# Two changes in a fused attention and feed-forward kernel: how float64 weights become float32, and where the probabilities are split

## The chip, the cores and the metric

One core of a Trainium2 chip. The metric is the device time of the program in microseconds, the median of the runs shown; less is better. The engines named below are TensorE (PE, with its weight loads PEld), VectorE (DVE), ScalarE (ACT), GpSimd (POOL) and SyncE (SP, which issues the DMA transfers).

## The reference, cut to what matters

```python
# q, k, v: [8, 8, 576, 64] float32;  w_a, w_b: [512, 1536], w_out: [1536, 512] float64
k_p = k.reshape(B, H, 72, 8, D).mean(axis=3)      # keys and values pooled by 8
v_p = v.reshape(B, H, 72, 8, D).mean(axis=3)
scores = scale * np.matmul(q, k_p.transpose(0, 1, 3, 2))
scores = scores - np.max(scores, axis=-1, keepdims=True)
attn = np.exp(scores)
attn = attn / (np.sum(attn, axis=-1, keepdims=True) + 1e-09)
x = np.matmul(attn, v_p)                          # heads side by side: [4608, 512]
out = ((x @ w_a) * (x @ w_b)) @ w_out             # [4608, 512] float32
```

The weights reach the chip as float64, so the kernel makes float32 out of their 64 bits itself.

## The kernel before, in words

Every float32 factor on TensorE is split into a high part, rounded to the short float32r format, and a low part, the remainder; a product is three products (high by high, low by high, high by low). So all of TensorE's operands are float32r.

The 4608 rows of x are made in 40 chunks of 128 or 64 queries (`chunk`) and multiplied in nine tiles of 512 rows. A tile takes twelve steps of the inner loop, one for 128 of the 1536 features: `ffn_in` (a and b, 24 products of 512 columns into `psa` and `psb`), `gated` (h = a * b on DVE, L530; split into `hh` on ACT and `hl` on DVE), and one step later `ffn_out` (twelve products into `acc`).

The order is written by hand. Chains of work (generators) are resumed slot by slot, about six slots a step; `yield n` continues n slots later, `yield PE` asks for a turn on TensorE between two groups of the inner loop's products. What one resumption issues goes to the engines' queues in that order, and each engine runs its queue in order.

The weights: `convert_weights` runs once for each of the three matrices and each of the twelve steps, 36 times, while the first tile is multiplied. SP loads the words of a step (`load_words`). ACT makes `low` (L211, the low word scaled) and `mag` (L212, the magnitude of the high word). DVE masks and shifts the high word (L213), puts the sign and the exponent's top bit back (L216), and multiplies by whether the magnitude reaches float32's normal range (L222, a slot later). POOL adds `low` (L226, another slot later). `split_weight`, for all nine tiles, makes the high part on ACT (L238) and the low part on POOL (L171 through `low_part`, tiles `jla`, `jlb`, `jlo`).

The probabilities: a chunk's scores `s` are exponentiated on ACT (L426), summed on DVE (L428, the factor is `z`, L430), and multiplied by `z` on POOL (L432; in two of the first four chunks on DVE). ACT copies the high parts into `pr` and `rem` (L441, L443; of 72 pooled keys 64 are handled pair of heads by pair of heads, the other 8 for four heads at once in `rem`), POOL makes the low parts (L171). `turn` then transposes on TensorE (L477): four transposes of the high half, a slot later four of the low half and two of the rest. ACT takes each of the three groups out of PSUM (L478). A block of chunks is multiplied with the values (L510 to L513, tile `po`), ACT takes the high part (L521) and DVE, a slot later, the low part (L523, in the profile L171 `xl`). Scores, transposes and these products share two PSUM buffers with the tag `att`.

Of the kernel before, what the change touches and what calls it, by code (L numbers as in the profile page):

```python
# [9 lines left out]
F32 = mybir.dt.float32  # L10
# [10 lines left out]
P = 128  # L21
# [6 lines left out]
# the high word of float64 2**-126, read as float32  # L28
MIN_HIGH = 2.0**-15 * 1.125
# [12 lines left out]
# of the pooled keys the first KM are multiplied with the values head pair by head pair, the KR  # L42
# that remain for four heads at a time: (hi, lo, hi) x 4 heads x KR rows
# [23 lines left out]
# the same before the first step: chunks one after the other, the values, the second batch's keys,  # L67
# the weights' loads and how much later their conversion begins
# [45 lines left out]
def attn_moe_kernel(ctx: ExitStack, tc: tile.TileContext, q, k, v, vr, wa, wb, wo, out):  # L114
# [12 lines left out]
    ident0 = tmp("ident0")[:, :P]  # L127
    make_identity(nc, ident0)
    ident = const.tile([P, P], F32R, name="ident")
# [43 lines left out]
    # the first batch's inputs wait where the last weights come later  # L173
# [21 lines left out]
    def convert_weights(name, j, first):  # L195
        """float64 bits to the nearest float32: the sign and the exponent's top bit stay, 27 bits of
        the high word move up by three, what lies below float32's normal range becomes zero, and
        the low word rounds into the last three bits"""
# [6 lines left out]
        for f in range(NF):  # L205
# [480 lines left out]
```

## Time and profile before

| | us |
|---|---|
| median of three runs (1107.82 to 1108.48) | 1107.91 |
| span of the profiled execution | 1107.4 |
| PE busy in it | 1038.7 |
| DVE busy | 611.5 |
| POOL busy | 618.8 |
| ACT busy | 522.9 |

The profiled execution is one run of the program; the span goes from its first to its last instruction. The shares of busy time are means over the whole span. The kernel has two stages with different limits, so the rows below are taken from each stage by itself: an opening of some 216 us, in which the weights are converted and the first tile is multiplied, and the rest.

### The profile page before, as it was taken

The numbers are of one execution on the slowest core, as the hardware profiler recorded it, in microseconds if no ns is written. First come the engines' busy times: TensorE is split into PE (matmuls) and PEld (weight loads), VectorE is DVE, ScalarE is ACT, GpSimd is POOL, SyncE is SP. The second block draws the span as 40 slices with busy tenths as digits, with TensorE's granted clock in tenths as the row PEclk, the third lists the DMA queues.
The fourth block names the chain that finished last, engine by engine and source line by source line (L and its number), as shares of the span: only waits on it lengthen the run. The fifth ranks groups of instructions, "written<-read, shape, count | busy, mean of one in ns | idle before, by whom it ended". The sixth has DMA issues, their size and how long they took to land.

```text
span 1107.4 us, 13650 instructions
## 1 busy us (share of the span) xinstructions
PE 1038.7 (94%) x4964; PEld 861.7 (78%) x4964; DVE 611.5 (55%) x917; ACT 522.9 (47%) x1051; POOL 618.8 (56%) x501
## 2 busy tenths in 40 slices
PE   4378887899999999999999999999999999999998
PEld 4356665688887888888888888888888888888887
DVE  7999999863348333753367335654458343332212
ACT  3655555544445445544455445444445444443332
POOL 6557776655555555555555455554556455554442
PEclk9989888999999999999999999999999999999999
DMA  6454344120023000400021002200211020001001
GB/s 220 128 154 126 105 145 131 48 89 1 1 71 110 1 1 22 148 3 1 1 94 59 1 1 91 82 1 1 69 55 49 1 67 1 1 1 38 1 1 38
DMA packets 29874, 59.59 MB, mean 54 GB/s; under 512 B 7120, under 2 KB 7120, under 8 KB 29808
## 3 DMA queue, kind: packets, MB, share of 16 engines
q1 hardware_dynamic: 29808, 58.73, 16.9%
q8 instruction: 39, 0.64, 0.3%
q14 instruction: 27, 0.22, 0.1%
HBM read 49.28 MB, written 9.44 MB: 53 GB/s over the span
## 4 chain that ended last, share of the span: by engine, by line
PE 81%; DVE 14%; issue 2%; DMA 1%; ACT 1%; POOL 0%; SPq 0%; DVEq 0%; POOLq 0%; ACTq 0%
PE acc L573 9%; PE psa L552 8%; PE psb L552 8%; PE acc L575 8%; PE acc L574 8%; PE psa L554 8%; PE psa L553 8%; PE psb L554 8%; PE psb L553 8%; PE ptr L477 2%; PE psc L406 2%; DVE wo_raw L216 1%; DVE wo_raw L213 1%; DVE wa_raw L222 1%; DVE wb_raw L216 1%
## 5 line engine op out<-in xcount | busy, mean ns | idle before, releaser
L171 POOL TENSOR_TENSOR jlb<-wb_raw,jhb 128x512 fp32r<-128x512 f32 x108 | 142.9, 1323 | 220.9 <-ACT jhb L238 220.9
L530 DVE TENSOR_TENSOR h<-psb,h 128x512 f32<-128x512 f32 x108 | 74.5, 690 | 343.6 <-PE psb L554 340.4
L171 POOL TENSOR_TENSOR jla<-wa_raw,jha 128x512 fp32r<-128x512 f32 x108 | 143.9, 1332 | 143.0 <-ACT jha L238 117.5
L557 ACT COPY h<-psa 128x512 f32<-128x512 f32 x108 | 63.5, 588 | 244.1 <-PE psa L554 235.4
L573 PE MATMUL acc<-jho,hh 128*128 128x512 f32 x432 | 175.5, 406 | 0.0
L552 PE MATMUL psb<-xh,jhb 128*128 128x512 f32 x432 | 172.4, 399 | 2.1 <-DVE h L530 2.1
L552 PE MATMUL psa<-xh,jha 128*128 128x512 f32 x432 | 173.7, 402 | 0.0
L554 PE MATMUL psb<-xh,jlb 128*128 128x512 f32 x432 | 170.0, 393 | 2.4 <-POOL jlb L171 2.4
L553 PE MATMUL psa<-xl,jha 128*128 128x512 f32 x432 | 170.0, 393 | 1.0 <-DVE xl L171 1.0
L554 PE MATMUL psa<-xh,jla 128*128 128x512 f32 x432 | 170.0, 394 | 0.0
L575 PE MATMUL acc<-jho,hl 128*128 128x512 f32 x432 | 170.0, 393 | 0.0
L574 PE MATMUL acc<-jlo,hh 128*128 128x512 f32 x432 | 169.9, 393 | 0.0
L553 PE MATMUL psb<-xl,jhb 128*128 128x512 f32 x432 | 169.6, 393 | 0.0
L171 POOL TENSOR_TENSOR jlo<-wo_raw,jho 128x512 fp32r<-128x512 f32 x108 | 155.1, 1437 | 5.6 <-ACT jho L238 5.6
L171 DVE TENSOR_TENSOR hl<-h,hh 128x512 fp32r<-128x512 f32 x108 | 95.1, 880 | 20.7 <-ACT hh L533 20.6
L533 ACT CAST hh<-h 128x512 fp32r<-128x512 f32 x108 | 67.1, 622 | 72.6 <-DVE h L530 72.6
L554 PEld LDWEIGHTS psb<-xh,jlb 128*128 128x128 f32 x432 | 82.0, 190 | 20.8 <-POOL jlb L171 3.3
L575 PEld LDWEIGHTS acc<-jho,hl 128*128 128x128 f32 x432 | 81.9, 190 | 18.2 <-DVE hl L171 0.3
L554 PEld LDWEIGHTS psa<-xh,jla 128*128 128x128 f32 x432 | 82.1, 190 | 17.8
L552 PEld LDWEIGHTS psb<-xh,jhb 128*128 128x128 f32 x432 | 81.9, 190 | 17.8 <-issue 2.5
L553 PEld LDWEIGHTS psa<-xl,jha 128*128 128x128 f32 x432 | 82.4, 191 | 16.6 <-DVE xl L171 1.5
L552 PEld LDWEIGHTS psa<-xh,jha 128*128 128x128 f32 x432 | 82.2, 190 | 15.3
(92 smaller groups left out, 1776.3 us busy)
## 6 DMA issues: line engine op xcount, KB each, us to landing
out<-y SPq DMA_DIRECT2D x36, 256.0 KB, 2.2
kraw<-in_k SPq DMA_DIRECT2D x28, 288.0 KB, 3.9
vraw<-in_v SPq DMA_DIRECT2D x28, 256.0 KB, 3.1
qraw<-in_q SPq DMA_DIRECT2D x28, 256.0 KB, 3.8
words<-in_wa SPq DMA_DIRECT2D x12, 512.0 KB, 3.7
words<-in_wb SPq DMA_DIRECT2D x12, 512.0 KB, 3.7
words<-in_wo SPq DMA_DIRECT2D x12, 512.0 KB, 3.6
vraw<-in_vr SPq DMA_DIRECT2D x14, 192.0 KB, 2.6
```

The source lines that it names most:

```text
L171: eng.tensor_tensor(out=lo, in0=src, in1=hi.bitcast(F32), op=ALU.subtract)
L216: nc.vector.scalar_tensor_tensor(out=wi, in0=hi, scalar=-(1 << 30), in1=wi, op0=ALU.bitwise_and, op1=ALU.bitwise_or)
L406: nc.tensor.matmul(pt[:n, :2 * hk], qh[:, g, :n], kd[:, g].rearrange("p w e s -> p (w e s)"), start=True, stop=False)
L530: nc.vector.tensor_tensor(out=h, in0=pt, in1=h, op=ALU.mult)
L533: nc.scalar.copy(hh, h)
L552: nc.tensor.matmul(pt, wh[:, c], xh[:, kk], start=(kk == 0), stop=False)
L553: nc.tensor.matmul(pt, wh[:, c], xl[:, kk], start=False, stop=False)
L554: nc.tensor.matmul(pt, wl[:, c], xh[:, kk], start=False, stop=(kk == NK - 1))
L557: nc.scalar.copy(h, pt)
L573: nc.tensor.matmul(acc[c], hh[:, cs], wh, start=(f == 0), stop=False)
L574: nc.tensor.matmul(acc[c], hh[:, cs], wl, start=False, stop=False)
L575: nc.tensor.matmul(acc[c], hl[:, cs], wh, start=False, stop=(f == NF - 1))
```

## The change

The weights: ACT makes `mag` first and then `low`. DVE takes the larger of the magnitude and 2^-15 and scales by 2^-16 (one instruction with one source), masks and shifts the result, a slot later puts the sign in and itself adds `low`. The multiplication by the comparison and POOL's add are gone. The next words are loaded a slot later than before, and the step is marked done a slot earlier.

The probabilities: the multiplication by `z` writes `pr` and three copies of the rest directly, in four instructions, in float32. The casts on ACT and the subtractions on POOL are gone. TensorE transposes float32 with a float32 identity, four transposes and later two. ACT takes the high part out of PSUM, and a slot later DVE subtracts it from the same PSUM tile to give the low part. The identity is no longer cast on DVE.

```diff
-            nc.scalar.activation(mag, hi.bitcast(F32), AF.Abs)
+            nc.scalar.activation(mag, hi.bitcast(F32), AF.Abs)
             nc.scalar.activation(low, lo.bitcast(U32), AF.Copy, scale=2.0**-29)
+            nc.vector.tensor_scalar(out=w, in0=mag, scalar1=TINY, scalar2=2.0**-16, op0=ALU.max, op1=ALU.mult)
             nc.vector.tensor_scalar(
-                out=wi, in0=hi, scalar1=0x07FFFFFF, scalar2=3, op0=ALU.bitwise_and, op1=ALU.logical_shift_left
+                out=wi, in0=wi, scalar1=0x0FFFFFFF, scalar2=3, op0=ALU.bitwise_and, op1=ALU.logical_shift_left
             )
+            yield 1
             nc.vector.scalar_tensor_tensor(
-                out=wi, in0=hi, scalar=-(1 << 30), in1=wi, op0=ALU.bitwise_and, op1=ALU.bitwise_or
+                out=wi, in0=hi, scalar=-(1 << 31), in1=wi, op0=ALU.bitwise_and, op1=ALU.bitwise_or
             )
             if f + 1 < NF:
                 load_words(f + 1)
-            yield 1
-            nc.vector.scalar_tensor_tensor(
-                out=w, in0=mag, scalar=MIN_HIGH, in1=w, op0=ALU.is_ge, op1=ALU.mult
-            )
-            yield 1
-            nc.gpsimd.tensor_tensor(out=wi, in0=wi, in1=low, op=ALU.add)
+            nc.vector.tensor_tensor(out=wi, in0=wi, in1=low, op=ALU.add)
             mark("weight", name, f)
...
-        (nc.vector if first and i % 2 else nc.gpsimd).tensor_tensor(
-            out=s[:n], in0=s[:n], in1=z[:n].unsqueeze(2).broadcast_to([n, H, SP]), op=ALU.mult
-        )
-        yield 1
...
-        nc.scalar.copy(pr[:n, 0], s[:n, :, :KM])
-        for x in (0, 2):
-            nc.scalar.copy(rem[:n, :, x], sr)
-        yield 1
-        low_part(nc.gpsimd, pr[:n, 1], s[:n, :, :KM], pr[:n, 0])
-        low_part(nc.gpsimd, rem[:n, :, 1], sr, rem[:n, :, 0])
+        eng = nc.vector if first and i % 2 else nc.gpsimd
+        eng.tensor_tensor(out=pr[:n], in0=s[:n, :, :KM], in1=zb.broadcast_to([n, H, KM]), op=ALU.mult)
+        for x in range(3):
+            eng.tensor_tensor(
+                out=rem[:n, :, x],
+                in0=s[:n, :, KM:].rearrange("p (r c) s -> p r c s", r=NG),
+                in1=zb.broadcast_to([n, H, KR]).rearrange("p (r c) s -> p r c s", r=NG),
+                op=ALU.mult,
+            )
         mark("probs", i)
+        yield 1
         yield PROBS_GAP
...
+            if x == 0:
+                for g in range(NK):
+                    src = pr[:n, 2 * g:2 * g + 2, :].rearrange("p a s -> p (a s)")
+                    nc.tensor.transpose(ptr[:, g, :n], src, ident[:n, :n])
+                nc.scalar.copy(th[:, :, cs], ptr[:, :, :n])
+                yield 1
+                low_part(nc.vector, tl[:, :, cs], ptr[:, :, :n], th[:, :, cs])
+            else:
+                for r in range(NG):
+                    src = rem[:n, r].rearrange("p a c s -> p (a c s)")
+                    nc.tensor.transpose(ptr[:NR, r, :n], src, ident[:n, :n])
+                nc.scalar.copy(tr[:NR, :, cs], ptr[:NR, :NG, :n])
+                yield 1
+                lo = slice(4 * KR, 2 * 4 * KR)
+                low_part(nc.vector, tr[lo, :, cs], ptr[lo, :NG, :n], tr[lo, :, cs])
```

## Rows read from the trace of the kernel before

**Rows 1.** The page's slices: busy tenths of PE and DVE in 40 equal slices.
```profile
PE 4378887899999999999999999999999999999998
DVE  7999999863348333753367335654458343332212
```

**Rows 2.** Table of stretches: us; busy PE, PEld, DVE, ACT, POOL; PEclk, DMA, GB/s.
```profile
68.00:208.00 140.00, 111.24 (x484) 87.75 (x485) 136.23 (x158) 74.73 (x150) 102.89 (x73) 0.85 0.39 118
...
216.00:1107.40 891.40, 887.51 (x4294) 739.66 (x4294) 409.10 (x659) 408.81 (x820) 473.00 (x381) 1.00 0.11 34
```

**Rows 3.** Timeline of PE, one chunk's transposes: start, us, what.
```profile
728.02 0.46 PE L477 MATMUL ptr<-ident,pr 128*128 128x128 f32 x4
728.31 0.47 PE L573 MATMUL acc<-jho,hh 128*128 128x512 f32 x1
728.62 0.39 PE L574 MATMUL acc<-jlo,hh 128*128 128x512 f32 x1
728.85 0.40 PE L575 MATMUL acc<-jho,hl 128*128 128x512 f32 x1
...
729.79 0.53 PE L477 MATMUL ptr<-ident,pr 128*128 128x128 f32 x4
730.16 0.30 PE L477 MATMUL ptr<-ident,rem 128*96 128x128 f32 x2
730.29 0.47 PE L573 MATMUL acc<-jho,hh 128*128 128x512 f32 x1
730.60 0.39 PE L574 MATMUL acc<-jlo,hh 128*128 128x512 f32 x1
```

**Rows 4.** Table of stretches, transposes (L477) alone, busy PE and PEld.
```profile
216.00:1107.40 891.40, 33.29 (x310) 31.38 (x310) 1.00 0.11 34
```

**Rows 5.** Timeline of DVE, the conversion without POOL beside it.
```profile
46.91 0.42 DVE L213 TENSOR_SCALAR wa_raw<-words 128x512 int32<-128x512 int32 x1
47.37 0.69 DVE L216 SCALAR_TENSOR_TENSOR wa_raw<-words,wa_raw 128x512 int32<-128x512 int32 x1
...
123.40 0.69 DVE L216 SCALAR_TENSOR_TENSOR wb_raw<-words,wb_raw 128x512 int32<-128x512 int32 x1
124.19 0.69 DVE L222 SCALAR_TENSOR_TENSOR wb_raw<-wmag_b,wb_raw 128x512 f32<-128x512 f32 x1
```

**Rows 6.** Timelines of DVE and of POOL, the conversion beside POOL.
```profile
97.56 1.65 DVE L216 SCALAR_TENSOR_TENSOR wo_raw<-words,wo_raw 128x512 int32<-128x512 int32 x1
...
97.19 1.47 POOL L171 TENSOR_TENSOR jlb<-wb_raw,jhb 128x512 fp32r<-128x512 f32 x1
```

**Rows 7.** Table of stretches, DVE of one line: L213, then L216, then L222.
```profile
68.00:208.00 140.00, 24.62 (x28) 0.85 0.39 118
...
68.00:208.00 140.00, 44.04 (x28) 0.85 0.39 118
...
68.00:208.00 140.00, 26.34 (x28) 0.85 0.39 118
```

**Rows 8.** Groups by line and shape, whole span: busy us, mean ns, idle before.
```profile
L171 POOL TENSOR_TENSOR pr<-s,pr 128x512 fp32r<-128x512 f32 x32 | 42.6, 1331 | 4.3 <-ACT pr L441 4.2
L432 POOL TENSOR_TENSOR s<-s,z 128x576 f32<-128x576 f32 x30 | 41.7, 1389 | 54.1 <-DVE z L430 34.9 <-ACT jha L238 19.2
...
L171 POOL TENSOR_TENSOR rem<-s,rem 128x64 fp32r<-128x64 f32 x32 | 12.7, 397 | 0.0
...
L171 DVE TENSOR_TENSOR xl<-po,xh 128x512 fp32r<-128x512 f32 x18 | 12.2, 688 | 10.1 <-ACT xh L521 10.1
...
L171 DVE TENSOR_TENSOR xl<-po,xh 128x256 fp32r<-128x256 f32 x2 | 0.8, 418 | 2.7 <-ACT xh L521 2.7
```

**Rows 9.** Table of stretches, POOL's adds (L226) alone.
```profile
68.00:208.00 140.00, 40.47 (x29) 0.85 0.39 118
```

**Rows 10.** Timelines of DVE and of ACT around 110 us.
```profile
110.31 0.41 DVE L213 TENSOR_SCALAR wo_raw<-words 128x512 int32<-128x512 int32 x1
...
110.41 0.66 ACT L211 ACTIVATE wlow_o<-words 128x512 int32<-128x512 uint32 x1
```

More of the change, by code (lines that the diff above doesn't have):

```diff
@@ L27 @@
 NK = DM // P
-MIN_HIGH = 2.0**-15 * 1.125
+TINY = 2.0**-15
 SCALE = 1.0 / float(D) ** 0.5
@@ L125, in tmp @@
         return sb.tile([P, 512], dtype, tag="tmp", name=name, bufs=NTMP)
-    ident0 = tmp("ident0")[:, :P]
-    make_identity(nc, ident0)
-    ident = const.tile([P, P], F32R, name="ident")
+    ident = const.tile([P, P], F32, name="ident")
+    make_identity(nc, ident)
     raw = {name: const.tile([P, NF, 512], F32, name=f"w{name}_raw") for name in ("a", "b", "o")}
@@ L431, in chunk @@
         yield 1
-        (nc.vector if first and i % 2 else nc.gpsimd).tensor_tensor(
-            out=s[:n], in0=s[:n], in1=z[:n].unsqueeze(2).broadcast_to([n, H, SP]), op=ALU.mult
-        )
-        yield 1
-        yield from wait(("turned", i - 2))
-        pr = sb.tile([P, 2, H, KM], F32R, tag="pr", name=f"pr_{i}")
-        rem = sb.tile([P, NG, 3, 4, KR], F32R, tag="rem", name=f"rem_{i}")
-        sr = s[:n, :, KM:].rearrange("p (r c) s -> p r c s", r=NG)
-        nc.scalar.copy(pr[:n, 0], s[:n, :, :KM])
-        for x in (0, 2):
-            nc.scalar.copy(rem[:n, :, x], sr)
-        yield 1
-        low_part(nc.gpsimd, pr[:n, 1], s[:n, :, :KM], pr[:n, 0])
-        low_part(nc.gpsimd, rem[:n, :, 1], sr, rem[:n, :, 0])
-        mark("probs", i)
+        yield from wait(("turned", i - 2))
+        pr = sb.tile([P, H, KM], F32, tag="pr", name=f"pr_{i}")
+        rem = sb.tile([P, NG, 3, 4, KR], F32, tag="rem", name=f"rem_{i}")
+        zb = z[:n].unsqueeze(2)
+        eng = nc.vector if first and i % 2 else nc.gpsimd
[7 more added lines that the diff above has]
+            )
+        mark("probs", i)
+        yield 1
         yield PROBS_GAP
@@ L454, in chunk @@
         total = sum(flat[c][2] for c in members)
-        if i == members[0]:
-            turned[j] = {}
-        def turn(x):
-            rows = P if x < 2 else NR
-            num = NK if x < 2 else NG
-            if x not in turned[j]:
-                if tile_of[i] < 2:
-                    turned[j][x] = sb.tile([P, num, BLOCK], F32R, tag=f"p{x}", name=f"p{x}_{j}", bufs=1)
-                elif x == 0:
-                    both = sb.tile([P, 2, NK, BLOCK_LATER], F32R, tag="work", name=f"p_{j}", bufs=1)
-                    turned[j].update({0: both[:, 0], 1: both[:, 1]})
-                else:
-                    turned[j][x] = sb.tile([P, NK * BLOCK], F32R, tag="p0", name=f"p{x}_{j}", bufs=1)[
-                        :, :NG * BLOCK_LATER
-                    ].rearrange("p (g s) -> p g s", g=NG)
-            dst = turned[j][x]
-            pt = ps.tile([P, 512], F32, tag="att", name=f"ptr_{i}_{x}", bufs=2)
-            ptr = pt.bitcast(F32R).rearrange("p (g s) -> p g s", g=NK)
-            for g in range(num):
-                src = pr[:n, x, 2 * g:2 * g + 2, :] if x < 2 else rem[:n, g]
-                src = src.rearrange("p a s -> p (a s)") if x < 2 else src.rearrange("p a c s -> p (a c s)")
-                nc.tensor.transpose(ptr[:rows, g, :n], src, ident[:n, :n])
-            nc.scalar.copy(dst[:rows, :, c0:c0 + n], ptr[:rows, :num, :n])
@@ L480, in chunk, with blocks_turned @@
-        yield from wait(("turned", i - 1), ("value", j - 1))
-        for x in range(3):
-            if x < 2 or t < 2:
+        def blocks_turned():
+            if tile_of[i] < 2:
+                both = [sb.tile([P, NK, BLOCK], F32R, tag=f"p{x}", name=f"p{x}_{j}", bufs=1) for x in range(2)]
+                rem = sb.tile([P, NG, BLOCK], F32R, tag="p2", name=f"p2_{j}", bufs=1)
+            else:
+                both = sb.tile([P, 2, NK, BLOCK_LATER], F32R, tag="work", name=f"p_{j}", bufs=1)
+                both = [both[:, 0], both[:, 1]]
+                rem = sb.tile([P, NK * BLOCK], F32R, tag="p0", name=f"p2_{j}", bufs=1)[
+                    :, :NG * BLOCK_LATER
+                ].rearrange("p (g s) -> p g s", g=NG)
+            return (*both, rem)
@@ new lines, in turn @@
+        def turn(x):
+            th, tl, tr = turned[j]
+            cs = slice(c0, c0 + n)
+            pt = ps.tile([P, 512], F32, tag="att", name=f"ptr_{i}_{x}", bufs=2)
+            ptr = pt.rearrange("p (g s) -> p g s", g=NK)
+            if x == 0:
[5 more added lines that the diff above has]
+                low_part(nc.vector, tl[:, :, cs], ptr[:, :, :n], th[:, :, cs])
+            else:
+                for r in range(NG):
[5 more added lines that the diff above has]
+                low_part(nc.vector, tr[lo, :, cs], ptr[lo, :NG, :n], tr[lo, :, cs])
@@ L483, in chunk @@
+        yield from wait(("turned", i - 1), ("value", j - 1))
+        if i == members[0]:
+            turned[j] = blocks_turned()
+        for x in range(2):
+            if x == 0 or t < 2:
                 yield PE
-            turn(x)
-            if x != 1 or t < 2:
-                yield 1
+            yield from turn(x)
         mark("turned", i)
@@ L497, in chunk @@
         per = min(NK, 512 // total)
-        th, tl, tr = (turned[j][x] for x in range(3))
+        th, tl, tr = turned[j]
         for g0 in range(0, NK, per):
@@ L589, in attn_moe_kernel @@
         load_early()
-        nc.vector.tensor_copy(ident, ident0)
         for t in kdiag + vdiag:
@@ L593, in attn_moe_kernel @@
         nc.vector.tensor_reduce(
-            out=mask[:NR], in_=ident0[:NR, :NR].rearrange("p (a c s) -> p c a s", a=3, c=4), axis=AX.XY, op=ALU.add
+            out=mask[:NR], in_=ident[:NR, :NR].rearrange("p (a c s) -> p c a s", a=3, c=4), axis=AX.XY, op=ALU.add
         )
```

## The prediction

> **What bounds the kernel now.** I read the page's slices first, then a table of stretches, then the timelines of single engines inside each stretch.
>
> The slices [rows 1] show two stages. For about the first fifth DVE stands at 9 in nearly every slice and PE wavers between 3 and 9; from there on PE is at 9 to the end and DVE falls to 2 to 7. The table of stretches [rows 2] says it in numbers: from 68 to 208 us DVE is busy 136.2 of 140 us and PE 111.2; from 216 us to the end PE is busy 887.5 of 891.4 us, DVE 409. So the two parts of the change meet two different limits. The weights' conversion lives only in the first stage, where DVE's time (and what makes its instructions long) sets the pace. The turning of the probabilities happens in both, but counts as TensorE time in the second and as DVE time in the first.
>
> What a transpose costs TensorE is read from the timeline of a chunk in the second stage [rows 3]. A 512-column product starts 0.23 us after the one before (728.62 to 728.85). The first four transposes start at 728.02 and the next product at 728.31, so four take 0.29 us, and the product behind them takes 0.31 instead of 0.23: 0.37 us in all. The second visit has four (729.79 to 730.16, 0.37 us) and two more (to 730.29), and again 0.08 us behind: 0.58 us. A mean transpose is thus (0.29 + 0.50) / 10 = 0.079 us. After 216 us there are 310 of them [rows 4], ten a chunk, so 31 chunks; the other nine lie in the first stage.
>
> Why DVE is slow in the first stage is read from single instructions. Undisturbed, the conversion's mask-and-shift (L213) takes 0.42 us and starts its successor after 0.46; the two-operand instructions L216 and L222 take 0.69 [rows 5]. Where an instruction of POOL runs, the same L216 takes 1.65 us, from 97.56, beside a POOL instruction that began at 97.19 [rows 6]. Over 68 to 208 us the three lines take 24.6, 44.0 and 26.3 us for 28 conversions [rows 7], 94.9 us together, where 28 x (0.42 + 0.69 + 0.69) would be 50.4. So 44.5 us are lost beside POOL's 73 instructions [rows 2], 0.61 us for each of them; hl and ql, of the same kind and on the same engine, lose some too, so I take 0.7.
>
> **The change part by part.**
>
> *The transposes, second stage.* Removed: four of ten transposes a chunk, the low half's, with their visit: 0.37 us [rows 3]. The visits of TensorE stay two, four transposes and later two, so the 0.08 us behind each stays as well. If a float32 transpose costs what a float32r one does, that is 31 x 0.36 = 11 us off a stage where PE has no idle time to hide it (0.36, as six of the chunks have 64 rows). No row shows a float32 operand on TensorE. From below I bound it by the cheapest row, 0.29 / 4 = 0.073 us, which brings the gain to 12 us; nothing speaks for less than that. From above I bound it by four times 0.079: the kernel itself splits a float32 operand into two parts, and two such operands make four products. I take the nearest row, the float32r transpose of the same 128 columns and four-byte elements. Two pages of the Trainium skill disagree here: "FP8 and Floating Point Precision", TensorE Precision Notes, gives true float32 four passes through the array, and "TensorE: Matmul & The Clock Gate", Terms, says that on trn2 a transpose mode makes float32 four times faster. By the first the sum would be the rival with four passes below, by the second it is the forecast. No run here shows it yet.
>
> *What goes from ACT and POOL, comes to DVE and waits, second stage.* ACT loses three casts and one of three evictions a chunk, POOL's three instructions of 1.39 + 1.33 + 0.40 us become one of about 1.33 and three of 0.40 [rows 8]. DVE gets two subtractions out of PSUM: the nearest rows are xl's of 128x512 and 128x256, 0.69 and 0.42 us [rows 8], so 1.1 us a chunk. None of this is on the path: DVE is busy 409 of 891 us [rows 2]. I cost it at nothing; the cover is that half-idle DVE. The wait that is added is that a PSUM buffer of the "att" pair comes free only after DVE's subtraction, a slot later. Behind it would queue the next chunk's scores or products on TensorE; but L521 and L523 already give the same buffers back in just this way (ACT, a slot, DVE). If the cover is gone, a wait of one subtraction a visit, 2 x 0.69 x 31 = 43 us, is the far bound; between nothing and that I take nothing, because PE shows no idle time behind the products that do the same.
>
> *The conversion, first stage.* 36 conversions. Removed from DVE: L222. Added to DVE: one single-operand instruction (maximum and scale) and the integer add that POOL had. Undisturbed: before 0.42 + 0.69 + 0.69, after 0.42 + 0.42 + 0.69 + 0.69, so +0.42. In addition the add now stands directly behind the instruction whose result it reads; in such a pair (123.40, 124.19) the second waits until 0.10 us after the first has ended [rows 5], which before was so for a part of the conversions only. I take +0.53 each: 36 x 0.53 = +19 us. Bounds: the new instruction at 0.42 (as L213) or at 0.69 (as the two-operand ones), 15 to 29 us.
>
> Removed from POOL: 36 adds; 29 of them in 68 to 208 us are busy 40.5 us [rows 9]. Each had DVE waiting 0.7 us: -25 us. Bounds: 0.61 each, -22; or all of a POOL instruction's 1.4 us, -50, which would need DVE to be standing at each of them and which the 0.61 contradicts.
>
> The order on ACT is turned so that the magnitude comes first; DVE now needs it at once, where before only the third instruction did. Mostly ACT is ahead. The worst kind is seen at 110.31: L213 starts before L211 (110.41, ending at 111.07), whose place the magnitude takes [rows 10]; DVE would stand 0.76 us, and hl, h and the other matrices' conversions stand behind it in its queue, on which TensorE waits. Six of the 36 conversions are late like this, together 3.6 us: +4. The load of the next words (SP's queue) is issued one slot later, behind the second bit instruction, and the release to the split comes one slot earlier; both move in DVE's own order, and neither is late as long as DVE is the bound: nothing.
>
> *The probabilities, first stage.* Nine chunks x 1.1 us of subtractions out of PSUM come onto the full DVE; adjoining instructions overlap a little, so +9. Two chunks multiply on DVE in four instructions instead of one, +1. POOL has 0.6 us less in each of seven chunks, -2.5. The identity's cast leaves DVE while the first inputs still load: nothing.
>
> Sum of the first stage: +19 - 25 + 4 + 9 + 1 - 2.5 = +5 us. That is a small difference of larger numbers, so I keep -8 to +14 for it. DVE stays the bound: the sum doesn't take it below TensorE's time.
>
> Against the profiled execution, whose span is 1107.4 us: 1107.4 - 11 + 5 = 1101.4; the median of the runs, 1107.91, lies 0.5 above the span: **1102 us**.
>
> **The rivals.**
>
> *Float32 transposes take several passes.* In its favour: the kernel writes float32r wherever TensorE reads, and no row has float32. Against: a transpose only moves data. With p us for one, the second stage changes by 31 x (6p - 0.79); with the +5 of the first stage the change loses from p = 0.105 us on. Two passes, 0.158: +5 + 5 = about 1118 us. Four, 0.316: 31 x (1.90 - 0.79) = +34, and +5, so 1147 us. If only the columns were repeated (0.23 / 4 = 0.057 us each), three more times for six transposes: 31 x 1.03 = +32, less the 11: 1134 us. This is the case that ends slower.
>
> *DVE gets no relief.* Without the adds, POOL's remaining instructions (three splits a step) could meet DVE as often, since DVE now has four instructions for three in the conversion. For it: the added time is of the kind that collides. Against it: POOL's busy time in the stage falls by two fifths. With half of the 25 us lost: 1102 + 12 = 1114 us.
>
> *Full relief.* If POOL's disappearance gives back more than 0.7 us each (1.1), the first stage ends 15 us earlier: 1087 us. Against it the 0.61 measured.
>
> *The removed transposes were hidden.* Then only the +5 remains: 1113 us. Against it stand 887.5 of 891.4 us.
>
> **How the numbers follow.** Forecast (one pass, first stage -8 to +14): 0.64, between 1090 and 1112. Several passes: 0.23, a third of it two passes. No relief: 0.06. Full relief: 0.04. Hidden: 0.03. Two passes, no relief and hidden stay inside a range up to 1127; four passes (0.15) and full relief are left out, so the range is 1090 to 1127. About 0.2%, 2.2 us, is what a measurement of this kernel can tell from no change. Inside the forecast I give 0.48 to faster than 1105.7, 0.10 to within, 0.06 to slower; with full relief faster is 0.52; slower has 0.06 + 0.23 + 0.06 + 0.03 = 0.38; same is 0.10.
>
> **What would show it.** In the profile after: ptr's x4 group followed by a product 0.29 to 0.37 us later (right), or over 0.6 (several passes); PE still full after the first stage; the point from which PE is full within some 10 us of 216; in the first stage L216-like instructions at 1.65 us less often; DVE still the busiest there. Wrong: transposes over 0.105 us, or a first stage that moves by more than 14 us, or idle PE behind "att" in the second stage.

## The result, and the profile after

| | before | after |
|---|---|---|
| median, us | 1107.91 | 1111.01 (1110.71 to 1115.67) |
| ratio to before | | 1.0039, 95% interval 1.0029 to 1.0048 |
| span of the profiled execution, us | 1107.4 | 1113.9 |
| end of the first tile (start of its last gate product on DVE, tile `h`), us | 223.4 | 220.3 |
| from there to the last gate product, us | 874.8 | 884.4 |

The change makes the kernel slower by 0.3 to 0.5%, where 0.5% faster was forecast. The profiled execution after is the longest of seven (1115.67 us), 4.7 us above their median, so its 6.5 us more span overstate a difference of medians of 3.1 us. In every run with both figures the time lies 1.7 to 2.0 us above the span, so the profiled execution of before (span 1107.4) lies some 1.4 us above its own median. The parts are still plain: the first tile ends 3.1 us earlier, and all that follows takes 9.6 us longer.

The page of after, busy tenths of PE and DVE and the granted clock in 40 slices, against [rows 1]:

```profile
PE   4477987899998999999999999999999999999998
DVE  7899999953466344764476445664567444442111
PEclk9788889999998999999999999999999999999999
```

The shape is the same, but PE has a slice of 8 in the thirteenth place, at the same place as a clock of 8: a hole in the stage that was full. The table of stretches (columns as in [rows 2]) shows how big it is:

```profile
68.00:208.00 140.00, 109.73 (x477) 87.00 (x478) 131.97 (x204) 71.06 (x136) 53.98 (x49) 0.88 0.39 119
216.00:1113.90 897.90, 883.60 (x4155) 732.00 (x4153) 444.77 (x714) 368.78 (x694) 459.95 (x412) 0.99 0.11 34
...
332.00:368.00 36.00, 31.01 (x136) 24.13 (x135) 23.54 (x40) 13.43 (x26) 16.73 (x17) 0.91 0.25 83
...
586.00:622.00 36.00, 33.45 (x155) 26.73 (x153) 23.13 (x42) 14.20 (x29) 19.89 (x22) 0.95 0.11 34
...
840.00:876.00 36.00, 33.45 (x167) 26.96 (x166) 23.37 (x44) 14.61 (x29) 20.40 (x22) 1.00 0.10 31
```

From 216 us PE is idle for 14.3 us, where it was 3.9 in [rows 2] (nearly all of it behind the last product). Three stretches hold nearly all that is new: 36 - 31.01 = 5.0 us, and twice 2.55. In two of them the granted clock fell as well: 36 x 0.09 = 3.2 us and 36 x 0.05 = 1.8 us of TensorE's time. Idle and clock together are 15.1 us. Each stretch holds two chunks of 64 rows that follow each other, one at the end of a batch and one at the start of the next. The scores of the first come directly behind the transposes of the 128-row chunk before it, and those of the second, some 15 to 19 us later, directly behind the transposes of the first.

What ends these waits stands in the table of waits after 218 us (us in total, times, longest):

```profile
PE psc L403 <- DVE p L170: 6.4, 5, 1.5
PEld psc L403 <- DVE s L409: 5.0, 6, 0.8
...
PE psc L403 <- DVE s L409: 3.7, 6, 0.6
```

The scores (`psc`) wait for one of the two `att` buffers, which DVE's new subtraction (`p`) still reads, or for the one buffer that is left to be read by the scores' own sum (`s`). The timeline of PE and DVE at the first place shows the order:

```profile
335.83 0.39 PE L561 MATMUL psb<-xh,jlb 128*128 128x512 f32 x1
...
336.06 0.38 PE L481 MATMUL ptr<-ident,rem 128*96 128x128 f32 x2
336.33 0.69 DVE L537 TENSOR_TENSOR h<-psb,h 128x512 f32<-128x512 f32 x1 [3.68 <-PE psb L561]
...
336.94 0.68 DVE L170 TENSOR_TENSOR p<-ptr,p 128x512 fp32r<-128x512 f32 x1
337.77 0.32 PE L403 MATMUL psc<-kdiag,qh 128*64 128x288 f32 x1 [1.32 <-DVE p L170]
...
338.76 0.50 PE L403 MATMUL psc<-kdiag,qh 128*64 128x288 f32 x1 [0.61 <-DVE s L409]
...
340.13 0.63 PE L582 MATMUL acc<-jho,hl 128*128 128x512 f32 x1
340.56 0.63 PE L580 MATMUL acc<-jho,hh 128*128 128x512 f32 x1
...
342.07 0.69 DVE L588 COPY y<-acc 128x512 f32<-128x512 f32 x1 [2.20 <-PE acc L582]
342.80 0.42 DVE L170 TENSOR_TENSOR p<-ptr,p 32x256 fp32r<-32x256 f32 x1
...
343.27 0.35 PE L403 MATMUL psc<-kdiag,qh 128*64 128x288 f32 x1 [0.91 <-DVE p L170]
```

Read it from the top. The last gate product goes to TensorE at 335.83, and right behind it the small transposes (336.06) and the scores, with no product between. DVE executes in order: it must first make `h`, which waits for that last product (3.68 us idle), and only then the subtraction that releases the first buffer. TensorE stands 1.32 us. The small transposes' own subtraction is a slot later again, at 342.80, behind a copy `y` that waits for further products; until then the scores have one buffer, and stand 0.61 and 0.91 us more. The products at 340.13 and 340.56 follow each other by 0.43 us instead of 0.23: after these waits the granted clock is at its lower level (1.2 GHz).

The kernel before has the same small transposes and the same kind of scores, but not side by side. Its timeline of PE for the same two chunks:

```profile
343.16 0.46 PE L477 MATMUL ptr<-ident,pr 128*128 128x128 f32 x4
...
343.45 0.30 PE L477 MATMUL ptr<-ident,rem 128*96 128x128 f32 x2
343.59 0.46 PE L552 MATMUL psa<-xh,jha 128*128 128x512 f32 x1
...
344.81 0.40 PE L554 MATMUL psa<-xh,jla 128*128 128x512 f32 x1
345.04 0.29 PE L406 MATMUL psc<-kdiag,qh 128*64 128x288 f32 x1
```

Between 343.59 and 345.04 stand six products, 1.45 us, in which ACT empties both buffers. The scores here are the second half of that chunk's; the first half came ahead of all its neighbour's transposes, from 339.57 on. In each slot of the inner loop first all chains that are due are resumed, and then one chain that asked with `yield PE` gets the turn. Before, the second visit (low half and small transposes) took that turn, so the scores had to wait for the next slot, six products later. In the change, after the second tile, the small transposes stand behind a `yield 1` and no `yield PE`: they are issued at the start of their slot without the turn, and the next chunk's scores take the turn directly behind them.

### The profile page after: what moved, and what is told of

Same layout as the page of the kernel before. It is cut to its first block, busy times and chain, and to the rows that moved or that the text cites. A ratio compares the mean times of both kernels' runs of the same rounds, so it can differ in the third digit from the quotient of the medians.

```text
span 1113.9 us, 13287 instructions
## 1 busy us (share of the span) xinstructions
PE 1037.6 (93%) x4804; PEld 855.6 (77%) x4804; DVE 640.9 (58%) x1038; ACT 472.9 (42%) x891; POOL 541.7 (49%) x499
## 4 chain that ended last, share of the span: by engine, by line
PE 78%; DVE 17%; issue 2%; DMA 2%; ACT 1%; POOL 0%; SPq 0%; DVEq 0%; POOLq 0%; ACTq 0%
PE psb L559 8%; PE acc L580 8%; PE psb L561 8%; PE psb L560 8%; PE acc L582 8%; PE acc L581 8%; PE psa L559 8%; PE psa L561 8%; PE psa L560 8%; PE psc L403 2%; PE ptr L474 1%; DVE hl L170 1%; DVE wo_raw L223 1%; DVE wb_raw L218 1%; DVE h L537 1%
## 5 line engine op out<-in xcount | busy, mean ns | idle before, releaser
L170 POOL TENSOR_TENSOR jla<-wa_raw,jha 128x512 fp32r<-128x512 f32 x108 | 153.0, 1417 | 120.1 <-ACT jha L235 110.2
L559 PE MATMUL psb<-xh,jhb 128*128 128x512 f32 x432 | 175.7, 407 | 2.1 <-DVE h L537 2.1
L170 DVE TENSOR_TENSOR hl<-h,hh 128x512 fp32r<-128x512 f32 x108 | 106.3, 985 | 9.3 <-ACT hh L540 8.5
```

Source lines behind the costliest of these rows:

```text
L170: eng.tensor_tensor(out=lo, in0=src, in1=hi.bitcast(F32), op=ALU.subtract)
L559: nc.tensor.matmul(pt, wh[:, c], xh[:, kk], start=(kk == 0), stop=False)
```

## The experiments

Every kernel was timed beside the kernel before, which had medians of 1107.77 to 1108.04 us. "First tile" and "rest" are the two last rows of the table above; "idle" is PE's idle time between the end of the first tile and the last product. The rest also holds what a lower granted clock took there: about 5 us in after and e2, 1.7 us in e4, e6 and e9, nothing in the others.

| run | median us | ratio, 95% interval | first tile | rest | idle |
|---|---|---|---|---|---|
| before | 1107.91 | | 223.4 | 874.8 | 0.1 |
| after | 1111.01 | 1.0039 (1.0029 to 1.0048) | 220.3 | 884.4 | 10.4 |
| e1_no_gap | 1105.83 | 0.9979 (0.9971 to 0.9988) | 219.5 | 874.2 | 6.0 |
| e2_probs_only | 1113.84 | 1.0055 (1.0039 to 1.0071) | 220.4 | 881.7 | 8.5 |
| e3_weights_only | 1110.77 | 1.0023 (1.0015 to 1.0032) | 223.8 | 874.9 | 0.1 |
| e4_fp32r | 1110.45 | 1.0029 (1.0019 to 1.0039) | 219.5 | 878.4 | 10.5 |
| e5_act_release | 1110.86 | 1.0022 (1.0014 to 1.0031) | 222.7 | 876.1 | 6.8 |
| e6_two_slots | 1123.66 | 1.0136 (1.0117 to 1.0154) | 228.4 | 882.6 | 11.0 |
| e7_pool_add | 1102.15 | 0.9944 (0.9931 to 0.9957) | 216.3 | 874.9 | 0.0 |
| e8_no_max | 1091.26 | 0.9849 (0.9836 to 0.9863) | 205.0 | 875.3 | 0.4 |
| e9_pool_add_no_gap | 1100.03 | 0.9927 (0.9915 to 0.9939) | 213.9 | 875.7 | 5.9 |
| e10_turn_earlier | 1097.71 | 0.9901 (0.9888 to 0.9914) | 211.5 | 873.7 | 5.6 |
| e11_before_wait | 1109.07 | 1.0013 (1.0003 to 1.0023) | 222.8 | 875.9 | 1.3 |
| e12_only_earlier | 1109.54 | 1.0019 (1.0010 to 1.0028) | 219.1 | 878.2 | 9.7 |

**e1_no_gap: the subtraction without its slot of delay**

```diff
     nc.scalar.copy(th[:, :, cs], ptr[:, :, :n])
-    yield 1
     low_part(nc.vector, tl[:, :, cs], ptr[:, :, :n], th[:, :, cs])
+    yield 1
...
     nc.scalar.copy(tr[:NR, :, cs], ptr[:NR, :NG, :n])
-    yield 1
     lo = slice(4 * KR, 2 * 4 * KR)
     low_part(nc.vector, tr[lo, :, cs], ptr[lo, :NG, :n], tr[lo, :, cs])
+    yield 1
```

> The changed kernel, with DVE's subtraction out of PSUM issued right behind ACT's copy instead of a slot later; nothing is left out. Theory A (TensorE waits for an att buffer that DVE gives back late, because the subtraction stands in DVE's queue behind the gate product, which itself waits for TensorE): TensorE's idle time after 218 us, 14 us in the changed kernel's profile, falls to 3 to 6, the steps at the meeting of two 64-row chunks (third, fifth and seventh tile) lose their 13 to 15 us lengths, and the time is 1097 to 1102 us. Theory B (a float32 transpose costs more than a float32r one): unchanged, 1110 to 1113. Theory C (the first stage got longer through the weights): unchanged as well.

Measured: 1105.83 us, 5.2 below the change, and faster than before. The direction is the one that only the wait explains; the size is less than expected, as 6.0 us of idle time stay. The timeline shows why:

```profile
335.27 0.38 PE L481 MATMUL ptr<-ident,rem 128*96 128x128 f32 x2
335.45 0.34 PE L403 MATMUL psc<-kdiag,qh 128*64 128x288 f32 x1
335.48 0.69 DVE L537 TENSOR_TENSOR h<-psb,h 128x512 f32<-128x512 f32 x1
...
336.20 0.42 DVE L170 TENSOR_TENSOR p<-ptr,p 32x256 fp32r<-32x256 f32 x1
...
336.67 0.35 PE L403 MATMUL psc<-kdiag,qh 128*64 128x288 f32 x1 [0.81 <-DVE p L170]
```

The large subtraction is out of the way, so the first scores start at once; the second ones still meet the buffer of the small transposes, filled 0.2 us before, and wait for its subtraction behind `h`. Issued directly behind ACT's copy, the subtraction still comes too late for scores that stand directly behind the transposes.

**e2_probs_only and e3_weights_only: each part alone.** In e2 the conversion, in e3 the probabilities are those of the kernel before. The core of e2 against the changed kernel; e3 has the same lines the other way round, against the kernel before:

```diff
-            nc.vector.tensor_scalar(out=w, in0=mag, scalar1=TINY, scalar2=2.0**-16, op0=ALU.max, op1=ALU.mult)
...
+            nc.vector.scalar_tensor_tensor(
+                out=w, in0=mag, scalar=MIN_HIGH, in1=w, op0=ALU.is_ge, op1=ALU.mult
+            )
...
-            nc.vector.tensor_tensor(out=wi, in0=wi, in1=low, op=ALU.add)
+            nc.gpsimd.tensor_tensor(out=wi, in0=wi, in1=low, op=ALU.add)
```

> The kernel before with the second part of the change alone (probabilities turned in float32, split on the way out of PSUM); the weights are converted as before. Theory A: the long steps at the meeting of two 64-row chunks are all there, and the first tile's last step, 3 us earlier in the changed kernel, comes at about its time before or up to 9 us later, since DVE gets nine chunks' subtractions without losing POOL's adds: 1112 to 1122 us. Theory B: 1110 to 1118 with transposes of over 0.105 us. Theory C: faster than before, 1098 to 1103.

> The kernel before with the first part of the change alone (weights without GpSimd); the probabilities as before. Theory A: only the first stage moves; by my sum -25 for POOL's adds, +19 for DVE's, +4 for the waits for the magnitude, so -2, and as the changed kernel's profile ends the first tile 3 us earlier with 9 us of subtractions more, rather -8 to -12: 1095 to 1106 us, with the steady part as before. Theory C: 1110 to 1118.

Measured: the probabilities alone bring the loss behind the first tile (881.7 against 874.8, with 8.5 us of idle time at the same three places) and a gain ahead of it (220.4 against 223.4, where about the old time or up to 9 us more was expected). The conversion alone leaves the rest as it was (874.9, idle 0.1), and costs 2.8 us by the medians of its round (1110.77 against 1107.98), where a gain was expected; the time falls into the range of theory C. So there are two losses, of different causes.

**e4_fp32r: the transposes' type.** `rem` and its transposes likewise.

```diff
-        pr = sb.tile([P, H, KM], F32, tag="pr", name=f"pr_{i}")
+        pr = sb.tile([P, H, KM], F32R, tag="pr", name=f"pr_{i}")
-                    nc.tensor.transpose(ptr[:, g, :n], src, ident[:n, :n])
+                    nc.tensor.transpose(ptr.bitcast(F32R)[:, g, :n], src, ident_r[:n, :n])
```

> The changed kernel with the probabilities, their rest and the identity written as float32r and transposed so, which leaves nothing for the low part (the subtraction runs all the same): it leaves out the low part's value and nothing of the work; one cast of the identity on DVE is added in the opening. It prices the type of the transposes by itself. Theory A: within 2 us of the changed kernel, four transposes followed by a product 0.29 to 0.37 us after their start in both. Theory B: 8 us or more below the changed kernel.

Measured: 1110.45 us and 10.5 us of idle time, within 0.6 us of the change by the medians. What float32 itself costs is read off the change's own products. Timeline of PE, the four large transposes, and two small ones of another chunk:

```profile
334.00 0.39 PE L561 MATMUL psb<-xh,jlb 128*128 128x512 f32 x1
334.24 0.60 PE L474 MATMUL ptr<-ident,pr 128*128 128x128 f32 x4
334.59 0.48 PE L559 MATMUL psb<-xh,jhb 128*128 128x512 f32 x1
334.90 0.40 PE L560 MATMUL psb<-xl,jhb 128*128 128x512 f32 x1
...
733.72 0.39 PE L561 MATMUL psb<-xh,jlb 128*128 128x512 f32 x1
733.95 0.38 PE L481 MATMUL ptr<-ident,rem 128*96 128x128 f32 x2
734.09 0.48 PE L580 MATMUL acc<-jho,hh 128*128 128x512 f32 x1
734.40 0.39 PE L581 MATMUL acc<-jlo,hh 128*128 128x512 f32 x1
```

Two products without a visit take 2 x 0.227 us; with four float32 transposes between them they take 0.90, so the visit costs 0.45 us, and the visit of two costs 0.68 - 0.45 = 0.23. With float32r the visit of four costs 0.37, in [rows 3] as in e4. A float32 transpose is thus dearer by about 0.02 us, not twice or four times as dear. By the median visit behind the first tile a chunk costs TensorE 0.45 + 0.23 = 0.67 us where it cost 0.37 + 0.51 = 0.89 (unrounded sums; the second visit in [rows 3], 0.58, is one of the dearer), and in e4 0.37 + 0.19 = 0.56. The type is so worth 0.11 us a chunk, some 3.3 us for 31 of them by these rows; the medians of the runs differ by 0.6 only, with executions of each that lie 5 to 6 us apart.

**e5_act_release: ACT empties the buffer.** The second visit likewise.

```diff
     nc.scalar.copy(th[:, :, cs], ptr[:, :, :n])
+    whole = tmp(f"whole_{i}_{x}").rearrange("p (g s) -> p g s", g=NK)
+    nc.scalar.copy(whole[:, :, :n], ptr[:, :, :n])
     yield 1
-    low_part(nc.vector, tl[:, :, cs], ptr[:, :, :n], th[:, :, cs])
+    low_part(nc.vector, tl[:, :, cs], whole[:, :, :n], th[:, :, cs])
```

> The changed kernel, but ACT copies the whole float32 PSUM tile of turned probabilities to SBUF right behind the copy of the high part, and DVE subtracts from SBUF a slot later, so the att buffer comes free by ACT alone. Theory A (the loss of the second stage is TensorE waiting for an att buffer that only DVE's late subtraction releases): TensorE's idle time after the first tile falls from 10.4 us to below 2, the steps at the three places where two 64-row chunks meet fall back to about 10 us, and the time to 1094 to 1101 us. Rival B (float32 transposes cost several passes): unchanged, 1109 to 1112. Rival C (DVE is the loaded engine and its added subtractions cost the time): unchanged or slower, 1111 to 1114, since DVE keeps every instruction.

Measured: 1110.86 us. No wait for DVE's subtraction is left, but 6.8 us of idle time are. The scores now stand 1.03 us at each of the three places for the second of ACT's two copies, with smaller waits of the same kind 4.0 us in all; the first of the three:

```profile
340.12 0.34 PE L403 MATMUL psc<-kdiag,qh 128*64 128x288 f32 x1 [1.03 <-ACT whole L487]
```

The expectation of under 2 us failed, and with it the first form of the theory, in which DVE's late release was the whole cause. With ACT as with DVE, scores directly behind the transposes wait. The rest did fall to 876.1 us; the first tile, at 222.7, took 2.4 us of that back with the added copies.

**e6_two_slots: a longer delay.** The second visit likewise.

```diff
     nc.scalar.copy(th[:, :, cs], ptr[:, :, :n])
-    yield 1
+    yield 2
```

> The changed kernel with two slots instead of one between ACT's copy and DVE's subtraction out of PSUM; nothing else. Theory A: each att buffer is held about 1.6 us longer, TensorE's idle time after the first tile grows from 10 to 15 to 30 us, and the time goes to 1116 to 1130 us. Rivals B and C (the transposes themselves, or DVE's load): the work of each engine is the same, so 1110 to 1112 us.

Measured: 1123.66 us, inside the expected range, but not for the expected reason: the idle time is 11.0 us, hardly more than with one slot, and 10.5 of them are waits for the scores' own sum `s`, none for the subtraction. The first tile ends at 228.4 instead of 220.3, and the rest takes no longer than in the change (882.6 against 884.4). So behind the first tile the wait hardly grows with the delay; why the first tile does was not followed up.

**e11_before_wait: the late release alone, in the kernel before**

```diff
-            nc.scalar.copy(dst[:rows, :, c0:c0 + n], ptr[:rows, :num, :n])
+            if x != 1 or t < 2:
+                nc.scalar.copy(dst[:rows, :, c0:c0 + n], ptr[:rows, :num, :n])
+                return None
+            return lambda: nc.vector.tensor_copy(dst[:rows, :, c0:c0 + n], ptr[:rows, :num, :n])
...
+        if t >= 2:
+            late()
```

> The kernel before, unchanged in its conversion, its transposes and its splits; only the copy of the turned low half out of PSUM is made by DVE and a slot later, from the third tile on, instead of by ACT at once. This puts the disputed wait into the kernel before by itself. Theory A (an att buffer that DVE releases late makes TensorE wait, at the places where two 64-row chunks meet): TensorE's idle time after the first tile rises from 0.1 to 5 to 15 us, at about 336, 590 and 844 us, and the time to 1113 to 1124 us. Rivals B and C (float32 transposes, or the added subtractions' own time): neither is in this kernel, so 1107 to 1109 us.

Measured: 1109.07 us, idle 1.3 us; 5 to 15 were expected. Only one of PE's waits behind the first tile is for the buffer (`p`):

```profile
PE psc L406 <- DVE p L481: 0.6, 1, 0.6
```

In this kernel, where six products stand between the transposes and the scores and only the low half's buffer is released late, that release costs almost nothing. This miss points to the missing half of the cause.

**e12_only_earlier: the place alone, in the changed kernel**

```diff
-        yield PROBS_GAP
+        yield PROBS_GAP if t < 2 else PROBS_GAP - 1
```

> The changed kernel with one number changed: from the third tile on, a chunk's transposes are issued one slot earlier. DVE's subtraction still comes a slot late and releases the att buffer, the add stays on DVE. Theory A2 (TensorE waits because the small transposes now stand directly ahead of the next 64-row chunk's scores, so that the scores need a buffer that has only just been filled; DVE's late release only lengthens that wait): TensorE's idle time after the first tile falls from 10.4 to 2 to 5 us, with waits for pr the largest part, the three steps of 13 to 15 us fall to 11 or less, and the time goes to 1100 to 1105 us. Theory A in its first form (the late release is enough by itself, wherever the scores stand): idle stays above 8 us and the time at 1108 to 1112 us.

Measured: 1109.54 us, 1.5 below the change. The table of waits of PE behind the first tile:

```profile
PE ptr L474 <- POOL pr L435: 6.0, 4, 2.2
PE psc L403 <- DVE p L170: 3.1, 3, 1.0
```

The scores' waits for `att` fall from 6.4 + 3.7 = 10.1 to 3.1 us, as the place would have it, but a new one comes: the transposes a slot earlier wait for POOL's multiplication four times, 6.0 us. The idle time therefore falls only to 9.7. These are the idle time and the time that were expected of the first form, but not by its mechanism, under which the waits for `att` would have stayed; the second form was right on where the waits go and far too low on what the wait for `pr` costs. Six products alone are not enough, as both buffers are released late here: the 3.1 us are three waits of 1.03 us for the second of them. The four kernels make a square. The waits for `att` are 10.1 us with the change's place and its late release (after), 5.1 with the early release alone (e1), 3.1 with the earlier place alone (e12), and none with both (e10, below; it also has the add on POOL, which changes nothing in these waits: they are 5.1 us in e9 as in e1). The cause is the two together: the small transposes directly ahead of scores that need both buffers, and a release that DVE's order delays.

**e7_pool_add and e8_no_max: the conversion taken apart.** Both against e3_weights_only, e7 first:

```diff
-            nc.vector.tensor_tensor(out=wi, in0=wi, in1=low, op=ALU.add)
+            nc.gpsimd.tensor_tensor(out=wi, in0=wi, in1=low, op=ALU.add)
```

```diff
-            nc.vector.tensor_scalar(out=w, in0=mag, scalar1=TINY, scalar2=2.0**-16, op0=ALU.max, op1=ALU.mult)
-                out=wi, in0=wi, scalar1=0x0FFFFFFF, scalar2=3, op0=ALU.bitwise_and, op1=ALU.logical_shift_left
+                out=wi, in0=hi, scalar1=0x07FFFFFF, scalar2=3, op0=ALU.bitwise_and, op1=ALU.logical_shift_left
...
-                out=wi, in0=hi, scalar=-(1 << 31), in1=wi, op0=ALU.bitwise_and, op1=ALU.bitwise_or
+                out=wi, in0=hi, scalar=-(1 << 30), in1=wi, op0=ALU.bitwise_and, op1=ALU.bitwise_or
```

> The kernel before with the new conversion (four instructions), but with the integer add given back to POOL; the probabilities as before. It prices the relief that the change should get from taking the adds off POOL, against the run with the new conversion alone (1110.8 us). As predicted (each add on POOL makes DVE wait 0.7 us, its own 0.53 saved): DVE waits 25 us more and works 19 us less, and the first stage also keeps the added instruction, so 1114 to 1120 us. Rival D (DVE had slack of its own in this stage, so that POOL's adds cost nothing on the path): 1108 to 1111 us. Rival E (the chain of one conversion, each instruction waiting for the one before it, sets the pace and not DVE's sum): one more crossing between engines a conversion, 1111 to 1114.

> The kernel before with the new conversion's order and its add on DVE, but without the added maximum-and-scale instruction (the bits are masked straight from the high word, as before); it leaves out the flush of values below float32's normal range. The probabilities as before. It prices that instruction and its wait for ACT's magnitude, against the run with the new conversion alone (1110.8 us). As predicted (0.53 us each for 36, and 4 us of waiting): 1086 to 1092 us. Rival D (DVE has slack in this stage, TensorE's own work or the loads set its end): 1105 to 1110. Rival E (the wait for the magnitude and not the instruction's own time is what costs): DVE's idle time in 68 to 208 us falls from 11 to below 5 us, and the time to 1100 to 1105.

Measured: the add back on POOL gives 1102.15 us, 8.6 faster than e3, where 3 to 9 slower was expected. Without the added instruction the time is 1091.26, 19.5 below e3 and inside what was expected as predicted. Rival E, that the wait for the magnitude costs and not the instruction, is out: DVE's idle time in 68 to 208 us is 11.2 us in e8 and 11.3 in e3, so it did not fall, and the time is far below 1100. Table of stretches for single lines of DVE, 28 to 224 us, all 36 conversions: e3_weights_only, maximum and scale, mask and shift, sign, add:

```profile
28.00:224.00 196.00, 19.98 (x36) 0.84 0.38 118
...
28.00:224.00 196.00, 22.23 (x36) 0.84 0.38 118
...
28.00:224.00 196.00, 31.92 (x36) 0.84 0.38 118
...
28.00:224.00 196.00, 38.43 (x36) 0.84 0.38 118
```

and e7_pool_add, the first three of them (the fourth is on POOL, 49.61 us):

```profile
28.00:224.00 196.00, 32.57 (x36) 0.92 0.38 118
...
28.00:224.00 196.00, 35.41 (x36) 0.92 0.38 118
...
28.00:224.00 196.00, 31.92 (x36) 0.92 0.38 118
```

With the adds on POOL the other three lines take 99.9 us, without them 74.1: a relief of 25.8 us, 0.72 for each add. But the add takes 38.4 us on DVE, 1.07 each, as it collides with POOL's remaining splits itself (undisturbed it takes 0.69). Moving the adds to DVE costs it 12.6 us in these four lines and moves the end of the first tile by 7.5; DVE's other instructions got shorter without the adds on POOL. Its whole account stands in the table of stretches (columns as in [rows 2]) from 68 us to 1.4 us before the first tile's end, for before, e3, e7 and e8:

```profile
68.00:222.00 154.00, 122.67 (x543) 97.18 (x544) 147.68 (x175) 81.28 (x162) 110.22 (x79) 0.87 0.37 113
...
68.00:222.40 154.40, 121.94 (x546) 97.53 (x545) 140.98 (x205) 81.96 (x164) 67.19 (x50) 0.86 0.36 114
...
68.00:214.90 146.90, 118.99 (x547) 95.27 (x546) 134.72 (x175) 81.66 (x162) 104.78 (x79) 0.90 0.39 120
...
68.00:203.60 135.60, 114.59 (x545) 91.00 (x544) 124.60 (x176) 81.30 (x162) 67.05 (x50) 0.94 0.41 129
```

From e3 to e7 DVE works 6.3 us less and stands 1.2 less, together the 7.5; from e3 to e8 it works 16.4 less and stands 2.4 less, together 18.8. From before to e3 it works 6.7 us less as well, but stands 7.1 us more (13.4 against 6.3), and the end stays.

The Trainium skill ("GPSIMD Engine Reference", 4.1 Engine selection) puts elementwise adds on VectorE and not on GpSimd; here, where VectorE is the bound, the 8.6 us decide against it. The Trainium skill's page "Perfetto Trace Analysis", Optimizing Scalar/DVE Operations, warns that moving work between those two might not help, as they share a read port. The relief of 0.72 us for each add agrees that they hold each other up, though here the moving did matter.

**e9_pool_add_no_gap and e10_turn_earlier: both losses taken out.** e9 against e1_no_gap, then e10 against e9:

```diff
-            nc.vector.tensor_tensor(out=wi, in0=wi, in1=low, op=ALU.add)
+            nc.gpsimd.tensor_tensor(out=wi, in0=wi, in1=low, op=ALU.add)
```

```diff
-        yield PROBS_GAP
+        yield PROBS_GAP if t < 2 else PROBS_GAP - 1
```

> The changed kernel with both costs that the runs so far point to taken out: the integer add given back to POOL, and DVE's subtraction issued directly behind ACT's copy. If the two terms are independent (the add on DVE costs 7.5 us of the first stage, by the end of the first tile in the profiles with the new conversion alone, 223.8 against 216.3 us; the late subtraction costs about 5 us of the median, 1111.0 against 1105.8): 1096 to 1100 us, faster than both kernels, with some 6 us of TensorE idle after the first tile. If the probabilities' subtractions out of PSUM need the DVE time that the adds on POOL disturb: 1101 to 1106 us.

> The kernel of the run before, with the transposes of a chunk issued one slot earlier from the third tile on, so that the small transposes no longer stand directly ahead of the next 64-row chunk's scores. Theory A (TensorE waits only where scores follow at once on a buffer that DVE still has to release): the waits of 0.81 us behind DVE's small subtraction disappear, TensorE's idle time after the first tile falls from 6 to 2 to 4 us, and the time is 1 to 4 us below that run. Rival (the multiplication on POOL is not ready a slot earlier): a wait for pr takes their place, at each chunk up to 1 us, and the time is 0 to 20 us above it.

Measured: 1100.03 and 1097.71 us, 0.7 and 1.0% faster than before. The two terms nearly add up: 1105.83 less 7.5 is 1098.3, 1.7 below e9. In e10 the wait for `att` behind DVE's small subtraction is gone, and what PE still waits for is this:

```profile
PE ptr L474 <- POOL pr L435: 4.0, 3, 1.4
PE psc L406 <- DVE ql L170: 0.6, 1, 0.6
```

The idle time is 5.6 us, above the 2 to 4 expected: the rival's wait for `pr` takes most of what the place gives back, and 2.3 us by the medians remain.

## Why the prediction was wrong, step by step

- *What bounds the kernel*: right. The conversion moved only the first tile (e3, e7, e8: 874.9 to 875.3 us behind it), and the probabilities moved the rest.
- *The added wait costs nothing*: this is the step that failed. It was costed by analogy: the values' products give the same buffers back late, "in just this way", and PE is not idle behind them. Two things were not read. The subtraction's place in DVE's queue: `h` and `y` ahead of it wait for TensorE, which waits for the subtraction. And the place of the transposes in TensorE's order: the prediction said that the visits stay two, but the second one no longer takes a slot's turn, and so it came to stand directly ahead of scores that need both buffers. Shown by e1, e11, e12 and e10 together; each alone gives only a part. Price in the profile: 10.3 us of idle time and 5.0 of clock, where nothing was put down and the far bound was 43 us. The profile is that of the longest execution, so in the median one the price is likely less.
- *The transposes, -11 us*: right in mechanism, mis-sized. Float32 costs a fifth more than float32r and no second pass; a chunk saves 0.22 us, not 0.36. The removed four are worth 0.32 by the median visits (0.89 against 0.56 in e4), and the type takes 0.11 of that back, which the sum had at nothing. By the rest of the kernels in which the waits are few, e1 (874.2 - 6.0) and e10 (873.7 - 5.6) against 874.7, it is about -6.5 us. Of the two pages of the Trainium skill set against each other there, "TensorE: Matmul & The Clock Gate", Terms, agrees with the 0.45 us for four; the four passes of "FP8 and Floating Point Precision", TensorE Precision Notes, would have made it more than 1 us (an estimate, 4 x 0.29 us of [rows 3]), and the trace does not show them for a transpose.
- *The conversion, -2 us (+19 - 25 + 4)*: close in the profile (+0.4 at the end of the first tile, e3), worse by the medians (+2.8). The two differ because the profiled execution of e3 lies 1.1 us below its median and that of before some 1.4 above its own. That the net comes near is partly luck, as the terms are off in opposite directions. The add takes 38.4 us of DVE, where 36 x 0.69 = 24.8 went into the +19. The relief of the other conversion lines, 25.8 us, is as costed. Putting the maximum in the place of L222, with the new order, took 13.0 us of DVE's work off from 68 us on alone (before to e7), where 36 x 0.27 = 9.7 was in the sum. The waits for the magnitude were 8.1 us in e3 (28 to 205 us: 2.8, 2.1 and 3.2 for the three matrices) and 3.2 in the whole change, against 4. "DVE stays the bound" held only in part: from before to e3 DVE's work falls by 6.7 us and the end does not move, as its idle time grows by 7.1. The magnitude's waits are of that size, but e8, which has none of them ahead of its first bit instruction, stands idle as long (11.2 us in 68 to 208), so what causes the idle time stays open. The added maximum itself costs 19.5 us by the medians (e8), for 20.0 us of busy time.
- *The probabilities in the first stage, +7.5 us*: wrong in sign, -3.0 (e2 against before). Two other pairs of profiles agree: -3.5 (after against e3) and -2.4 (e9 against e7). Up to the eleventh step of the first tile e2 is between 1.3 us ahead of the kernel before and 2.2 behind it; the twelfth gains 3.2 us at once. DVE's nine chunks of subtractions do not add to the end as the sum had it. Which of the removed instructions gives that last step its gain was not tried, and stays open.
- *The sum*: 1107.4 - 3.1 + 10.3 + 5.0 - 5.7 = 1113.9, with the transposes as what is left over. Left out of it stays the spread: the change's executions lie between 1110.7 and 1115.7 us, those of before beside it within 0.7. The clock's 5.0 us in the profiled one are of that size, but whether the drop is what differs between executions was not shown; the second longest (1114.32 us) has the highest mean granted clock of the seven, 0.983. The forecast's last step, that the median lies 0.5 us above the span, compared two different executions; it moved the forecast by little.
- *What would show it*: the prediction named "idle PE behind att in the second stage" as a sign of being wrong, and that is the row that came.

## What to carry to other kernels

A buffer of a pair shared by several users is not free because the average engine is half idle: ask what stands ahead of the releasing instruction in its own engine's queue, whether that waits for the engine that wants the buffer, and what stands directly behind the filling instruction. When a diff moves a `yield`, write down TensorE's new order at the places where chunks meet before pricing anything. And cost an instruction that goes to a contended engine at its disturbed duration, 1.07 and not 0.69 us, even when its departure relieves that same engine.

## What the runs showed of the hardware

- A transpose of float32 costs TensorE about 0.02 us more than one of float32r (0.45 against 0.37 us for four). At this price the split can be made behind it.
- The integer add on DVE appears as a custom operation on 128x1024 elements of 16 bits. It takes 0.69 us by itself and 1.4 to 3.1 beside POOL, like the two-operand instructions of [rows 6].
- The same waits do not always lower the granted clock: it was 0.91 over 332 to 368 us, 0.95 over 586 to 622 and 1.00 over 840 to 876, with idle times of 5.0, 2.55 and 2.55 us. In e1, where waits were up to 2.0 us, it stayed at 1.00 in all three; in e9, with the same waits (5.9 against 6.0 us of idle time), it fell behind the wait of 2.0 us, to 0.95 over 325 to 361 us.
